# Token-order Q, one store per output block, and dummy matmuls in a convolution and token-mixing kernel

## The chip, the cores and the metric

The kernel runs on one core of one Trainium2 chip. The metric is the device time of one execution in microseconds; the median of three runs stands for a version. The engines are TensorE (PE; PEld is its weight load), VectorE (DVE), ScalarE (ACT), GpSimd (POOL) and SyncE (SP), which here only issues DMAs.

## The reference

Two steps follow one another on x of 8 batches x 4224 tokens x 192 channels (float32).

```python
# 1: causal convolution over 7 tokens, softmax weights, one set per head (24 channels each)
w = exp(weight - max); w = w / sum(w)
x_unf = x_pad[:, idx, :].reshape(B, S, K, H, group)
out = np.einsum('hk,bskhg->bshg', w, x_unf)
# 2: token mixing on that result (call it x again)
wq = x @ w_q;  wk = x @ w_k                       # 192 -> 64
W_tok = scale * np.einsum('bsd,btd->bst', wq, wk) # no softmax, no mask
mixed = np.einsum('bst,btd->bsd', W_tok, x)
out = np.maximum(mixed, 0.0) @ w_out
```

Nothing non-linear stands between the products of step 2, so the kernel never forms the 4224 x 4224 matrix: mixed = Q (w_k^T (x^T x)) scale, with a 192 x 192 Gram matrix per batch.

## The kernel before, in words

Each batch is cut into two halves of HALF = 2112 tokens, and each half into 18 chunks of 120 tokens (the last has 72). One job of each kind, for batch b:

- **Loads** (`load`, lines 192 to 210): GpSimd issues seven DMAs per batch, in three groups of semaphores, which cast x to bf16 on the way; a chunk comes with six tokens ahead of it. First rows and the short last chunks must be zero, which memsets do once (lines 247 to 252 and 359 to 363).
- **Y** (`job_y`, 406): the convolution as a product with a band matrix. Eight jobs per batch: g = 0, 1 is the first or second nine chunks of both halves, hp a pair of heads. Two matmuls of 432 columns, evicted to Y with one instruction, or three.
- **TD** (`job_td`, 449): the Vector engine transposes Y in 32 x 32 blocks, six instructions per batch.
- **Q** (`job_q`, 466): Q^T = w_q^T Y^T, two jobs per batch (g), 48 pairs of matmuls into four PSUM banks. Bank i holds tokens 32 i to 32 i + 31 of every chunk. The evictions (lines 485 to 514) copy bank i as it stands into columns 512 i on of QT: QT is therefore not in token order but has, for each i, all chunks' 32-token pieces behind each other, and the leftovers of the last chunks fill the gaps. Three eviction instructions for g = 0, eight for g = 1.
- **G** (`job_g`, 523): 18 jobs of three matmuls add up the Gram matrix in bank 7. **GEV, TR, MM** (539 to 576) evict it, transpose a part and multiply it with w_k to M.
- **Z** (`job_zd`, `job_zs`, 598 to 626): M times a block of 512 columns of QT (the fifth block is 64), then ReLU into a ring of NZ = 3 buffers.
- **O** (`job_o`, 628): Z times w_out. Output row r of a block takes every fourth column, so a partition holds four successive columns of QT for each half. Two jobs per block fill one buffer of a ring of NO = 8, and `then` (654 to 687) issues its stores. Since QT isn't in token order, a block's 512 columns lie in 16 stretches of 32 tokens: blocks 0 to 2 take one store per half, block 3 three per half (96, 30 and 2 partitions), the rest block one per half. The last block of the run is stored in two parts.

The order is not written out by hand. A planner (lines 697 to 865) holds streams of jobs, estimates when each could start (`ready`: free banks, ends of producers, `x_at` for the loads), and takes the ready job with the lowest due time; a due time is the batch number plus an offset and a slope from KEYS (lines 15 to 18). Each eviction goes to ScalarE or VectorE, whichever the planner's costs say is done first. The result is one fixed instruction list per engine, in which an instruction waits only for its semaphores. `free`, `x_at` and the `end` times set at lines 711 to 720 are the planner's picture of the start: TensorE free at 8.6 us, the third load group of batch 0 there at 12.0, the weights (`wos`) at 12.0. Nothing on the chip corrects them.

At the start TensorE runs 22 matmuls on zeros (`warm`, 388). The Vector engine builds the band matrix (lines 269 to 323), then runs three memsets (`z_later`, 359 to 363), on which GpSimd's loads of batch 1 wait (`load_all(1, z_later)`, 374). Behind those loads GpSimd casts the weights (`wos`, 375 to 386).

Of the kernel before, what the change touches and what calls it, by code (L numbers as in the profile page):

```python
# [12 lines left out]


KEYS = {
    "Y": (-0.34, -0.09), "T": (-0.03, 1.21), "Q": (0.23, 0.82), "G": (-0.01, 0.83),
    "Z": (0.93, 1.25), "O": (1.37, 0.86),
}


# [93 lines left out]
def bass_lightweight_conv__then__hypermixer_token_mlp_kernel(  # L114
# [8 lines left out]
    B, S, D = x.shape  # L123
# [5 lines left out]
    x_t, out_t, w_t = x.tensor, out.tensor, weight.tensor  # L129
# [4 lines left out]
    HALF = S // 2  # L134
    CW = 120
    NCK = 18
    LAST = HALF - 17 * CW
# [11 lines left out]
    P = Program(nc, es)  # L149
# [90 lines left out]
    def dve(fn, deps=()):  # L240
        return P.op("dve", fn, deps)
# [9 lines left out]
    z_band = dve(lambda e: e.memset(BAND[:, :, :], 0.0))  # L251
    z_wall = dve(lambda e: e.memset(WALL[:, :], 0.0))

    load(0, 0, 1, 8, xg[0][0])
    load(0, 1, 0, 9, xg[0][1])
    load(0, 0, 0, 1, xg[0][0], z_first)
# [78 lines left out]
    def twice(ap):  # L335
# [20 lines left out]
        ),  # L356
        [z_id],
    )
    z_later = [
        dve(lambda e: e.memset(shorts[:, 1:], 0.0)),  # L360
        dve(lambda e: e.memset(XW[0:6, 1:, 0, :], 0.0)),
        dve(lambda e: e.memset(ZT[:, :, :, 64:128], 0.0)),
    ]

    def load_all(b, deps):
        load(b, 0, 0, 1, xg[b][0], deps)
# [19 lines left out]
    wos.append(pool(lambda e: e.memset(M_SB[:, :, :], 0.0), [wos[-1]]))  # L386

    def warm(e):
        for i in range(22):
            last = e.matmul(PS[:, 0, :], WARM[:, 0:128], WARM[:, :], start=True, stop=True)  # L390
        return last

# [73 lines left out]
    def job_q(b, g):  # L466


        def pe(e, bk):
            for j in range(6):  # L470
                for i in range(4):
                    r = slice(32 * i, 32 * i + 32)
                    for h in range(2):
                        at_ = 64 * (j // 2 if h == 0 else (4, 5, 3)[j // 2]) + j % 2
                        rhs = YB[r, g, :, at_ : at_ + 63 : 2]
                        last = e.matmul(PS[64 * h : 64 * h + 64, bk + i, 0:288], WQ[r, j, :], rhs,  # L476
                                        start=j == 0, stop=j == 5, skip_group_check=True)
            return last

        def at(i, c):
            return 512 * i + (32 if i < 3 else 24) * c

        n = 9 if g == 0 else 7
        evacs = []
        for i0, i1 in ((0, 2), (2, 3), (3, 4)):

            def make(bk, i0=i0, i1=i1):
                q0 = (b % 2) * HALF  # L490
                w = 32 if i0 < 3 else 24

                def piece(p0, n_, o0, step):

                    if i1 - i0 == 2:
                        return (bass.AP(QT, q0 + o0, [[2 * HALF, 128], [step, 2], [1, n_]]),
                                PS[:, bk + i0 : bk + i1, p0 : p0 + n_])
                    return (QT[:, b % 2, o0 : o0 + n_], PS[:, bk + i0, p0 : p0 + n_])

                if i0 < 3:  # L500
                    r = [piece(0, 32 * n, at(i0, 9 * g), 512)]
                else:
                    o = QT[:, b % 2, at(3, 9 * g) : at(3, 9 * g) + 24 * n]
                    i = PS[:, bk + 3, 0 : 32 * n].rearrange("p (c w) -> p c w", w=32)
                    r = [(o.rearrange("p (c w) -> p c w", w=24), i[:, :, 0:24])]
                if g == 1:
                    r.append(piece(224, w, 1920 + 32 * i0, 32))
                    if i0 == 0:
                        r.append(piece(256, 32, 2048, 32))
                    if i0 == 2:  # L510
                        r.append(piece(256, 8, 2040, 0))
                return r

            evacs.append((make, ("Q", b, g, i0), (i1 - i0) * (n + 2 * g) * 32, False, "copy"))
# [69 lines left out]
    def zspan(i):  # L584
        return (512 * i, 512 if i < 4 else HALF - 2048)

    def zreads(b, i):
        s0, w = zspan(i)
        k = (0, 0, 2, 3, 3)[i]
        q = [("Q", b, 1, 0), ("Q", b, 1, 2)] if i > 2 else []  # L590
        return [("M", b), ("Q", b, 0, k), ("Q", b, 1, k)] + q

    def zring_after(n):
        bb, k = divmod(n - NZ, 5)
# [33 lines left out]
    def job_o(b, i, q):  # L628
        n = nth(b, i)
        zr, orr = n % NZ, n % NO  # L630
        rem = i == 4

        def pe(e, bk):
            kw = dict(skip_group_check=True)
            for j in range(1 if rem else 2):
                r = 2 * q + j
                cols = slice(0, 128) if rem else slice(r, 512, 4)
                o = PS[:, bk + j, :]
                for h in range(2):
                    e.matmul(o[:, 192 * h : 192 * h + 192], ZT[:, zr, h, cols], WO1,  # L640
                             start=h == 0, stop=False, **kw)
                last = e.matmul(o[:, 0:384], ZT[:, zr, 2, cols], WO2, start=False, stop=True, **kw)  # L642
            return last

        def make(bk):
            if rem:
                return [(OUT[0:64, orr, :, 0:192],
                         PS[0:64, bk, 0:384].rearrange("p (h d) -> p h d", h=2))]
            return [(
                OUT[:, orr, :, 384 * q : 384 * q + 384].rearrange("p h (r d) -> p r h d", r=2),  # L650
                PS[:, bk : bk + 2, 0:384].rearrange("p r (h d) -> p r h d", h=2),
            )]

        def then():
# [4 lines left out]
            row = lambda h, t: (b * S + h * HALF + t) * D  # L659
            chunk = [[4 * D, 8], [1, 4 * D]]  # L660
            for h in range(2):
                if rem:
                    parts = [(0, 64, row(h, 17 * CW), [[D, 64], [1, D]])]
                elif halves:
                    parts = [(0, 128, row(h, 32 * i + 2 * q),
                              [[CW * D, 16], [4 * D, 8], [1, 2 * D]])]
                elif i < 3:
                    parts = [(0, 128, row(h, 32 * i), [[CW * D, 16]] + chunk)]
                else:
                    parts = [  # L670
                        (0, 96, row(h, 96), [[CW * D, 16], [4 * D, 6], [1, 4 * D]]),
                        (96, 126, row(h, 16 * CW), [[4 * D, 30], [1, 4 * D]]),
                        (126, 128, row(h, 17 * CW + 64), [[4 * D, 2], [1, 4 * D]]),
                    ]
                for p0, p1, at, dims in parts:
                    src = OUT[p0:p1, orr, h, 0 : D if rem else 4 * D]
                    if halves:
                        src = OUT[:, orr, h, 2 * q * D : 2 * q * D + 2 * D]
                    st = P.dma(
                        "sp",  # L680
                        lambda e, src=src, at=at, dims=dims: e.dma_start(
                            bass.AP(out_t, at, dims), src
                        ),
                        og[orr], evs,
                    )
# [22 lines left out]
    head = {s: 0 for s in streams}  # L708


    free = {"pe": 8.6, "act": 8.5, "dve": 8.8}
    banks = [[0.0, []] for _ in range(8)]
    x_at = {}
    for b in range(B):
        for g in range(3):
            x_at[id(xg[b][g])] = (9.5, 9.5, 12.0)[g] if b == 0 else 3.0 + 9.2 * b + (3.0, 6.0, 9.5)[g]
    for o in band + [ident] + wqs:
        o.end = 8.5
    for o in wos:
        o.end = 12.0  # L720

    def ready(job):
        for r in job.reads:
# [119 lines left out]
    while True:  # L843
# [58 lines left out]
```

## Time and profile before

| | |
|---|---|
| median of three runs | 175.79 us (175.15 to 176.15) |
| profiled execution | 175.42 us |
| its span, first to last instruction | 173.7 us |
| mean granted TensorE clock | 0.964 |
| stores issued by SyncE | 114, 25.95 MB written to HBM |

The 1.7 us between the span and the execution's own time lie around the instructions that the profile shows. In rows of the timeline the first number is the start, the second the length, x the number of merged instructions, and the bracket the idle time of the engine before them with what ended it. A row of the groups ends with busy us and mean ns of one instruction, then idle time before them. A row of a stretch has its length, each engine's busy time and number of instructions, then the granted clock, the busy share of the DMA engines (above one where the transfer times of several queues overlap on an engine) and the rate. Rows of waits end with the sum, the number of times and the longest.

### The profile page before, as it was taken

The page shows a single profiled execution, that of the slowest core. Times are in us where ns is not written, and L with a number is a line of the kernel's source. Part 1 is how long each engine was busy: PE and PEld are TensorE (multiplying, and loading weights), DVE is VectorE, ACT ScalarE, POOL GpSimd, SP SyncE. Part 2 cuts the span into 40 slices and gives each one's busy share as a digit, 9 for nine tenths or more (in the row PEclk, how much of TensorE's full clock was granted, in tenths as well). Part 3 has the DMA queues.
Part 4 walks back from the last instruction along what each step waited for, and adds up shares of the span by engine and source line. Part 5 has one row for each costly group of instructions (what it writes and reads, how often), then busy time and mean ns, then how long its engine had stood idle before and what let it go on. Part 6 is the DMA issues. An engine that isn't in the chain of part 4 may idle for free.

```text
span 173.7 us, 4729 instructions
## 1 busy us (share of the span) xinstructions
PE 152.9 (88%) x1934; PEld 105.5 (61%) x1934; DVE 129.9 (75%) x246; ACT 126.0 (73%) x257; POOL 46.6 (27%) x74
## 2 busy tenths in 40 slices
PE   7755989999989999999999999999999999999400
PEld 2213855776758666766677677757676767766300
DVE  4883969948986899589967997699769976877200
ACT  2562479768987799679966997789768987698500
POOL 7839899999842300000000000000000000000000
PEclk9975999999999999999999999999999999999985
DMA  2999999999999999999999999992859266896697
GB/s 37 185 191 175 191 190 192 190 193 296 265 283 256 280 307 198 313 274 318 226 287 278 310 257 283 281 337 81 251 151 277 70 205 184 225 311 216 204 304 240
DMA packets 48933, 40.43 MB, mean 233 GB/s; under 512 B 39088, under 2 KB 40976, under 8 KB 48912
## 3 DMA queue, kind: packets, MB, share of 16 engines
q0 software_dynamic: 36992, 13.83, 66.9%
q1 hardware_dynamic: 11920, 26.30, 46.1%
q8 instruction: 15, 0.25, 0.5%
q14 instruction: 6, 0.05, 0.1%
HBM read 28.00 MB, written 25.95 MB: 311 GB/s over the span
## 4 chain that ended last, share of the span: by engine, by line
PE 61%; ACT 15%; DVE 9%; POOL 6%; issue 3%; ACTq 0%; POOLq 0%; DVEq 0%
PE ps L413 11%; PE ps L640 10%; PE ps L642 9%; PE ps L476 8%; ACT o_sb L805 6%; ACT zt L808 6%; PE ps L603 6%; PE ps L527 5%; PE ps L528 5%; PE ps L618 3%; PE ps L529 3%; POOL xw L205 3%; ACT y L805 3%; DVE yb L803 2%; DVE y L805 2%
## 5 line engine op out<-in xcount | busy, mean ns | idle before, releaser
L805 ACT COPY o_sb<-ps 128x768 f32<-128x768 f32 (+1 forms) x62 | 46.7, 777 | 6.7 <-PE ps L642 6.2
L640 PE MATMUL ps<-wall,zt 128*128 128x192 bf16 x272 | 45.0, 247 | 0.1
L642 PE MATMUL ps<-wall,zt 128*128 128x384 bf16 x136 | 44.3, 326 | 0.0
L805 ACT CAST y<-ps 128x864 bf16<-128x864 f32 (+3 forms) x58 | 32.5, 617 | 9.0 <-PE ps L413 8.6
L413 PE MATMUL ps<-xw,band 126*128 126x432 bf16 x128 | 32.0, 364 | 5.7 <-DMA xw<-in_x_dram 4.9
L810 DVE TENSOR_SCALAR zt<-ps 128x512 bf16<-128x512 f32 (+1 forms) x47 | 29.2, 634 | 9.6 <-PE ps L603 4.7
L808 ACT ACTIVATE zt<-ps 128x512 bf16<-128x512 f32 (+1 forms) x73 | 33.9, 535 | 1.5 <-PE ps L603 1.4
L640 PEld LDWEIGHTS ps<-wall,zt 128*128 128x128 bf16 x272 | 27.8, 113 | 10.8 <-issue 1.9
L527 PE MATMUL ps<-y 128*128 128x192 bf16 x144 | 34.1, 248 | 0.0
L528 PE MATMUL ps<-y 128*128 128x192 bf16 x144 | 34.0, 247 | 0.0
L803 DVE STREAM_TRANSPOSE yb<-y 128x576 int32<-128x576 int32 x48 | 33.5, 748 | 0.3
L805 DVE CAST y<-ps 128x864 bf16<-128x864 f32 (+3 forms) x38 | 29.7, 815 | 4.6 <-PE ps L413 4.1
L205 POOL DMA_DIRECT2D xw<-in_x_dram x32 | 30.1, 993 | 6.9 <-issue 6.0
L529 PE MATMUL ps<-y 128*128 128x128 bf16 x144 | 31.6, 220 | 0.0
L603 PE MATMUL ps<-qt,m_sb 128*128 128x512 bf16 (+1 forms) x80 | 25.6, 343 | 2.3 <-ACT zt L808 2.1
L805 ACT CAST qt<-ps 128x64 bf16<-128x64 f32 (+4 forms) x34 | 11.8, 403 | 14.3 <-PE ps L476 14.2
L805 DVE CAST qt<-ps 128x224 bf16<-128x224 f32 (+6 forms) x54 | 12.4, 288 | 11.3 <-PE ps L476 11.3
L413 PEld LDWEIGHTS ps<-xw,band 126*128 126x128 bf16 x128 | 10.4, 100 | 16.4 <-ACT band L318 3.1
L528 PEld LDWEIGHTS ps<-y 128*128 128x128 bf16 x144 | 14.2, 99 | 6.7 <-issue 0.2
L527 PEld LDWEIGHTS ps<-y 128*128 128x128 bf16 x144 | 14.2, 98 | 3.2 <-issue 0.4
L476 PE MATMUL ps<-yb,wq 32*64 32x288 bf16 x768 | 15.5, 286 | 0.2 <-DVE yb L803 0.2
L642 PEld LDWEIGHTS ps<-wall,zt 128*128 128x128 bf16 x136 | 15.2, 112 | 0.0
(63 smaller groups left out, 131.6 us busy)
## 6 DMA issues: line engine op xcount, KB each, us to landing
out_dram<-o_sb SPq DMA_DIRECT2D x46, 384.0 KB, 4.4
xw<-in_x_dram POOLq DMA_DIRECT2D x24, 384.0 KB, 19.3
out_dram<-o_sb SPq DMA_DIRECT2D x16, 288.0 KB
xw<-in_x_dram POOLq DMA_DIRECT2D x8, 432.0 KB, 18.0
out_dram<-o_sb SPq DMA_DIRECT2D x16, 90.0 KB
out_dram<-o_sb SPq DMA_DIRECT2D x16, 48.0 KB, 5.6
out_dram<-o_sb SPq DMA_DIRECT2D x4, 192.0 KB
xw<-in_x_dram POOLq DMA_DIRECT2D x16, 29.2 KB, 22.7
```

What stands on the lines that cost most here:

```text
L205: return e.dma_start(XW[0:rows, b % NX, slot : slot + n, :], bass.AP(x_t, base, [[D, rows], [CW * D, n], [1, D]]),)
L413: last = e.matmul(PS[:, k + j, 0:432], BAND[0 : 6 + CW, h, :], rhs, start=True, stop=True)
L476: last = e.matmul(PS[64 * h : 64 * h + 64, bk + i, 0:288], WQ[r, j, :], rhs, start=j == 0, stop=j == 5, skip_group_check=True)
L527: e.matmul(PS[:, 7, 0:192], y[:, 0:128], y[:, 0:192], start=c == 0, **fl)
L528: e.matmul(PS[:, 7, 192:384], y[:, 256:384], y[:, 192:384], start=False, **fl)
L529: return e.matmul(PS[:, 7, 384:512], y[:, 128:256], y[:, 128:256], start=False, **fl)
L603: return e.matmul(PS[:, bk, 0:w], M_SB[:, b % 2, 256 * h : 256 * h + 128], QT[:, b % 2, s0 : s0 + w], start=True, stop=True)
L640: e.matmul(o[:, 192 * h : 192 * h + 192], ZT[:, zr, h, cols], WO1, start=h == 0, stop=False, **kw)
L642: last = e.matmul(o[:, 0:384], ZT[:, zr, 2, cols], WO2, start=False, stop=True, **kw)
L803: last = e.transpose(o, i)
L805: last = e.copy(o, i) if eng == "act" else e.tensor_copy(o, i)
L808: last = e.activation(o, i, AF.Relu)
```

## The change

- QT is written in token order: the evictions of Q spread each bank's 32-token pieces with a stride of 120. Seven eviction instructions per batch instead of eleven. Z of a block then needs Q of the first nine chunks (blocks 0 and 1), of both (block 2), or of the second (3 and 4).
- A block of output is 512 successive tokens of each half, so one store per block takes both halves (two, of half the width, for the last block of the run).
- The two memsets of `z_later` on the x buffers move ahead of the band matrix; the third one stays, and the loads of batch 1 no longer wait for it.
- 32 matmuls on zeros instead of 22 at the start. While no G job has been placed, the planner fills any gap of TensorE over 0.3 us with a matmul on zeros, counted as 0.22 us, which waits for the band matrix.
- KEYS, `free`, `x_at` and the `end` times have other numbers.

```diff
-    "Y": (-0.34, -0.09), "T": (-0.03, 1.21), "Q": (0.23, 0.82), "G": (-0.01, 0.83),
-    "Z": (0.93, 1.25), "O": (1.37, 0.86),
+    "Y": (-0.34, 0.43), "T": (-0.12, 1.03), "Q": (0.02, 0.45), "G": (-0.01, 0.79),
+    "Z": (0.76, 1.54), "O": (1.57, 0.83),
...
     z_wall = dve(lambda e: e.memset(WALL[:, :], 0.0))
+    z_later = [
+        dve(lambda e: e.memset(shorts[:, 1:], 0.0)),
+        dve(lambda e: e.memset(XW[0:6, 1:, 0, :], 0.0)),
+    ]
...
-    z_later = [
-        dve(lambda e: e.memset(shorts[:, 1:], 0.0)),
-        dve(lambda e: e.memset(XW[0:6, 1:, 0, :], 0.0)),
-        dve(lambda e: e.memset(ZT[:, :, :, 64:128], 0.0)),
-    ]
+    dve(lambda e: e.memset(ZT[:, :, :, 64:128], 0.0))
...
-        for i in range(22):
+        for i in range(32):
...
+                n = 9 if g == 0 or i0 == 0 else 8
+                def piece(c, n_, w_):
+                    o = bass.AP(
+                        QT, (b % 2) * HALF + (9 * g + c) * CW + 32 * i0,
+                        [[2 * HALF, 128], [32, i1 - i0], [CW, n_], [1, w_]],
+                    )
+                    i = PS[:, bk + i0 : bk + i1, 32 * c : 32 * c + 32 * n_]
+                    i = i.rearrange("p i (c w) -> p i c w", w=32)[:, :, :, 0:w_]
+                    return (o, i) if i1 - i0 > 1 else (o[:, 0], i[:, 0])
+                r = [piece(0, n, w)]
+                if g == 1 and i0 == 2:
+                    r.append(piece(8, 1, LAST - 64))
...
-        k = (0, 0, 2, 3, 3)[i]
-        q = [("Q", b, 1, 0), ("Q", b, 1, 2)] if i > 2 else []
-        return [("M", b), ("Q", b, 0, k), ("Q", b, 1, k)] + q
+        gs = ((0,), (0,), (0, 1), (1,), (1,))[i]
+        return [("M", b)] + [("Q", b, g, k) for g in gs for k in (0, 2, 3)]
...
+            each, lo, hi = (1, 0, D) if rem else (4, 0, 4 * D)
+            if halves and not rem:
+                lo, hi = 2 * q * D, 2 * q * D + 2 * D
+            rows = 64 if rem else 128
+            to = bass.AP(
+                out_t, (b * S + 512 * i) * D + lo,
+                [[each * D, rows], [HALF * D, 2], [1, hi - lo]],
+            )
+            src = OUT[0:rows, orr, :, lo:hi]
+            st = P.dma("sp", lambda e: e.dma_start(to, src), og[orr], evs)
...
-    free = {"pe": 8.6, "act": 8.5, "dve": 8.8}
+    free = {"pe": 9.9, "act": 9.9, "dve": 9.9}
...
-            x_at[id(xg[b][g])] = (9.5, 9.5, 12.0)[g] if b == 0 else 3.0 + 9.2 * b + (3.0, 6.0, 9.5)[g]
+            x_at[id(xg[b][g])] = (10.0, 10.0, 14.8)[g] if b == 0 else 5.0 + 9.5 * b + (4.0, 6.5, 11.0)[g]
     for o in band + [ident] + wqs:
-        o.end = 8.5
+        o.end = 9.9
     for o in wos:
-        o.end = 12.0
+        o.end = 20.0
...
         s = best[1]
+        if head["G"] == 0 and best[2] > free["pe"] + 0.3:
+            P.op("pe", lambda e: e.matmul(PS[:, 7, :], WARM[:, 0:128], WARM[:, :], start=True,
+                                          stop=True), band)
+            free["pe"] += 0.22
+            continue
         place(streams[s][head[s]], best[2])
```

More of the change, by code (lines that the diff above doesn't have):

```diff
@@ L478, in pe @@
             return last
-        def at(i, c):
-            return 512 * i + (32 if i < 3 else 24) * c
-        n = 9 if g == 0 else 7
         evacs = []
@@ L489, in make @@
             def make(bk, i0=i0, i1=i1):
-                q0 = (b % 2) * HALF
                 w = 32 if i0 < 3 else 24
[L493 to L511, printed above, removed]
-                return r
-            evacs.append((make, ("Q", b, g, i0), (i1 - i0) * (n + 2 * g) * 32, False, "copy"))
+                n = 9 if g == 0 or i0 == 0 else 8
[10 more added lines that the diff above has]
+                    r.append(piece(8, 1, LAST - 64))
+                return r
+            evacs.append((make, ("Q", b, g, i0), (i1 - i0) * (32 if i0 < 3 else 24) * 9, False,
+                          "copy"))
         return Job(
@@ L587, in zreads @@
     def zreads(b, i):
-        s0, w = zspan(i)
-        k = (0, 0, 2, 3, 3)[i]
-        q = [("Q", b, 1, 0), ("Q", b, 1, 2)] if i > 2 else []
-        return [("M", b), ("Q", b, 0, k), ("Q", b, 1, k)] + q
+        gs = ((0,), (0,), (0, 1), (1,), (1,))[i]
+        return [("M", b)] + [("Q", b, g, k) for g in gs for k in (0, 2, 3)]
     def zring_after(n):
@@ L658, in then @@
             evs = [o for k in range(q if halves else 0, q + 1) for o in made[("OUT", b, i, k)]]
[L659 to L685, printed above, removed]
+            each, lo, hi = (1, 0, D) if rem else (4, 0, 4 * D)
[8 more added lines that the diff above has]
+            st = P.dma("sp", lambda e: e.dma_start(to, src), og[orr], evs)
             st.end = max(o.end for o in evs) + 5.0
```

## The prediction

> **What bounds the kernel now.** I read the page first, then busy time by stage, then the two ends of the run in the timeline.
>
> ```profile
> span 173.7 us, 4729 instructions
> PE 152.9 (88%) x1934; PEld 105.5 (61%) x1934; DVE 129.9 (75%) x246; ACT 126.0 (73%) x257; POOL 46.6 (27%) x74
> ...
> core 0: us, PE busy (x) PEld busy (x) DVE busy (x) ACT busy (x) POOL busy (x), PEclk, DMA share, GB/s
> 10.00:15.00 5.00, 2.62 (x9) 0.83 (x10) 3.29 (x5) 1.88 (x4) 3.34 (x5) 0.58 1.38 179
> 15.00:20.00 5.00, 5.00 (x40) 3.63 (x39) 3.50 (x5) 2.76 (x5) 4.49 (x12) 0.73 1.55 189
> 20.00:60.00 40.00, 38.07 (x576) 26.53 (x574) 32.02 (x59) 31.43 (x68) 32.08 (x43) 1.00 1.47 234
> 60.00:150.00 90.00, 88.54 (x1191) 63.50 (x1192) 75.45 (x140) 74.19 (x154) 0.00 (x0) 1.00 1.05 246
> 154.00:159.00 5.00, 4.95 (x38) 2.97 (x36) 4.09 (x9) 4.42 (x10) 0.00 (x0) 1.00 0.90 278
> 159.00:165.00 6.00, 3.45 (x31) 2.62 (x30) 2.14 (x3) 3.82 (x6) 0.00 (x0) 1.00 0.62 182
> 166.00:170.00 4.00, 0.00 (x0) 0.00 (x0) 0.00 (x0) 0.00 (x0) 0.00 (x0) 0.73 0.99 344
> ```
>
> The 88% hides three stages. From 60 to 150 us TensorE is busy 88.54 of 90 us: it is the bound there, and five batches of 18 us leave it 1.46 us idle, 0.29 a batch. From 10 to 20 us it is not: it is idle 2.38 us and its granted clock is 0.58 and then 0.73. At the end no engine computes any more, yet the run goes on for ten microseconds. The stores explain those:
>
> ```profile
> 152.54 1.18 SPq L681 DMA_DIRECT2D out_dram<-o_sb  x2
> 154.29 16.66 SPq L681 DMA_DIRECT2D out_dram<-o_sb  x24
> 165.25 5.70 SPq L681 DMA_DIRECT2D out_dram<-o_sb  x6
> L681 SPq DMA_DIRECT2D out_dram<-o_sb x114: 236/587/1444, 36.2 to 170.4; - x114
> DMA to landing us min/median/max: 3.3/4.9/7.2
> out_dram<-o_sb SPq DMA_DIRECT2D x16, 90.0 KB
> out_dram<-o_sb SPq DMA_DIRECT2D x16, 6.0 KB
> 152.76 1.50 ACT L805 COPY o_sb<-ps 128x768 f32<-128x768 f32 x2 [0.25 <-PE ps L642]
> 156.12 1.53 DVE L805 COPY o_sb<-ps 128x768 f32<-128x768 f32 x2 [0.18 <-PE ps L642]
> 159.81 1.51 ACT L805 COPY o_sb<-ps 128x768 f32<-128x768 f32 x2
> 161.18 0.96 DVE L805 COPY o_sb<-ps 128x768 f32<-128x768 f32 x1 [1.00 <-PE ps L642]
> 161.83 1.50 ACT L805 COPY o_sb<-ps 128x768 f32<-128x768 f32 x2 [0.51 <-PE ps L642]
> ```
>
> The last eviction ends at 161.83 + 1.50 = 163.33, but SyncE issues its last 24 stores without a pause from 154.29 to 170.95. A store occupies it for 0.59 us in the median, hardly less for 90 KB in 30 rows than for a half block of 384 KB. While it works through the many small ones (159 to 165) the DMA engines are 0.62 busy and move 182 GB/s; once only half blocks come (166 to 170) they are 0.99 busy at 344. So the tail is first a queue of issues on SyncE, and only then a transfer at full rate.
>
> **The merged stores.** Per batch 3 x 2 + 6 + 2 = 14 stores become five; the total falls from 114 to 41 (5 x 8, and one more for the halved last block). Bytes and the longest run (four tokens, 3,072 bytes) stay. No row shows an issue of 256 runs. Its bounds are 0.59 us (30 rows cost what 128 do) and twice that, 1.2; I take 0.6, and even 1.2 is under the transfer's own time, so it costs nothing here. Rework the queue with the evictions where they are. A block of 786 KB at 344 GB/s takes 2.29 us, a remainder block of 98 KB 0.29. A half block needs 1.14 us of transfer and lands 3.3 us after its issue at the least, so about 2.2 us are fixed (estimate). Transfers end: batch 6's block 2, issued at 152.54, at 157.0; block 3, ready at 154.26, at 159.3; remainder 159.6; batch 7's block 3, ready at 157.65, at 162.1 (159.85 + 2.29); remainder 162.4; block 0, ready at 160.61, at 165.1; block 1 (162.14) at 167.4; block 2 (162.63 and 163.33) at 169.7. That is 4.0 us before 173.7. The last block goes in runs half as long, so I take 3.7. At 278 GB/s over 0.90 busy, 309, the same chain ends at 170.7: gain 3.0. The best case is a last store that lands 4.9 us after 163.33, at 168.2: 5.5. The bound from below is zero, in the first rival. Earlier in the run the list of waits names no engine that waits for a store (the output ring is eight deep), so the other saved issues count nothing.
>
> **The start.**
>
> ```profile
> 1.25 6.26 PE L390 MATMUL ps<-warm 128*128 128x512 bf16 x22 [1.25 <-DVE warm L247]
> 1.31 2.06 POOL L205 DMA_DIRECT2D xw<-in_x_dram  x2 [0.81 <-POOLq L887]
> 4.30 1.78 POOL L205 DMA_DIRECT2D xw<-in_x_dram  x2
> 2.40 0.51 DVE L252 MEMSET wall<- 128x544 uint32 x1
> 4.40 0.17 DVE L270 TENSOR_TENSOR bits<-bits 128x5 int32<-128x5 int32 x1 [1.49 <-POOL bits L261]
> 9.71 0.86 DVE L360 MEMSET xw<- 128x960 uint32 x1 [0.26 <-issue]
> 10.60 0.46 DVE L361 MEMSET xw<- 6x480 uint32 x1
> 11.07 0.30 DVE L362 MEMSET zt<- 128x288 uint32 x1
> 12.58 1.06 DVE L805 CAST y<-ps 128x864 bf16<-128x864 f32 x1 [0.30 <-PE ps L413]
> 10.14 2.40 PE L413 MATMUL ps<-xw,band 126*128 126x432 bf16 x8 [2.63 <-DMA xw<-in_x_dram]
> 14.78 2.34 PE L413 MATMUL ps<-xw,band 126*128 126x432 bf16 x6 [2.24 <-DMA xw<-in_x_dram]
> 11.66 0.54 POOL L201 DMA_DIRECT2D xw<-in_x_dram  x1 [3.44 <-DVE zt L362]
> 16.93 2.72 POOL L328 CAST wall<-wst 128x192 bf16<-128x192 f32 x7
> ```
>
> TensorE stands idle for 2.63 us after the 22 warm-up matmuls and for 2.24 us until the third load group of batch 0 lands, and works at half clock between and after. Ten more warm-ups cost between the planner's 0.22 each and the mean of the 22, 6.26 / 22 = 0.285: they end at 9.7 to 10.4 instead of 7.51, against a start at 10.14. At worst that is 0.2 late, and 2 us late if they ran at half clock; the wait until 14.78 covers either.
>
> Clock: at 0.73 from 15 to 20 us, 5.00 x 0.27 = 1.35 us are lost on work that TensorE does without a gap; the dummies keep it occupied from 10 to 14.8, and I count 1.35.
>
> Fill: the planner's arrival of the third group goes from 12.0 to 14.8 (real: 14.78), so the Gram matmuls of chunks 0 to 8 are put ahead of the Y jobs of that group. They need all four evictions of the first half, which end at 12.58 + 1.06 = 13.64; with the two memsets gone from 9.71 the Vector engine can begin 0.3 earlier, say 13.3. That leaves 1.5 us before 14.78 for real work: 1.5.
>
> Given back: with work drawn forward, TensorE meets the reduction chain Gram, transpose, M of batch 0 with less to do beside it; it was idle 1.93 of 40 us between 20 and 60 already. I charge 0.6. The start then brings 1.35 + 1.5 - 0.6 = 2.25; bounds 0 (second rival) and 1.35 + 1.5 + 1.0 = 3.85, if half of the 1.93 goes too.
>
> The memsets: 0.86 + 0.46 = 1.32 us move in front of the first `bits` operation, where the Vector engine now idles 1.49 us for GpSimd: free by 0.17 us, and without that cover the band matrix would be up to 1.32 late. GpSimd issues loads at that moment. Two issues beside memsets took 2.06 us, two without 1.78, so I expect 0.1 to 0.3 of delay, inside the estimate of 13.3. [...]
>
> The loads of batch 1 no longer wait 3.44 us. GpSimd passes seven load issues; the weight casts behind them (16.93) wait for weights that SyncE asks for only at 9.6, so they and the loads of batch 2 behind them stay put. The DMA share of 1.38 against 1.55 shows a hole of at most 0.6 us in the load stream that this closes; batch 1 comes that much earlier, with TensorE otherwise occupied. I count nothing, bounds 0 and 0.6.
>
> **The steady part.**
>
> ```profile
> L805 ACT CAST qt<-ps 128x64 bf16<-128x64 f32 (+4 forms) x34 | 11.8, 403 | 14.3 <-PE ps L476 14.2
> L805 DVE CAST qt<-ps 128x224 bf16<-128x224 f32 (+6 forms) x54 | 12.4, 288 | 11.3 <-PE ps L476 11.3
> PEld ps L603 <- ACT zt L808: 3.6, 5, 0.7
> ```
>
> Q's evictions go from 11 to 7 instructions a batch: 88 in 24.2 us now, so four fewer of the short kind save at most 4 x 0.29 = 1.2 us of ScalarE and VectorE per batch. Neither is the bound (75 and 74 of 90 us), so this counts nothing; were they the bound it would be a gain. Writing tokens in runs of 32 instead of whole rows could cost from nothing to the mean of one Q eviction per batch, also covered. The new due times reorder every batch. The ceiling of a gain is the 0.29 idle a batch, 2.0 over seven; no row bounds the loss, which is the third rival. I take 0.4 of gain.
>
> Sum against the profiled execution, 175.42 us (span 173.7 and 1.7 around it): 175.4 - 3.7 - 2.25 - 0.4 = 169.1. The median of the three runs is 175.79, 0.37 above it: 169.4.
>
> **Rivals.** *The tail is bytes, not issues.* For it: from 165.25 on, six issues take 5.70 us, 0.95 each against 0.59, so they are pushed back by full engines. Against it: 159 to 165. If the engines take the two-half stores at the 246 GB/s of the steady part, a block costs 3.2 us and the same chain ends no earlier than now, at 174.7; the gain is nil: 175.8 - 2.65 = 173.1. [...] Chance 0.12.
>
> *The start brings nothing*, because dummies are laid at planned, not real times, or the clock drops anyway, or the lead is lost waiting for batch 1 and the weights: 175.8 - 3.7 - 0.4 = 171.7. The idle 1.93 between 20 and 60 speaks for it. Chance 0.16.
>
> *Slower: the reordering starves TensorE.* Z of a batch is now due at 0.76, but its ring of three buffers is freed by the second output job of block 2 of the batch before, due at 1.57 + 0.83 x 5/9 = 2.03, that is 1.03 on the same scale. Z jobs then come overdue and in bursts of three, and wait for evictions with the output jobs behind them. Now such a wait costs 0.7 us once a batch (3.6 over five). It decides from (3.7 + 2.25) / 7 = 0.85 us more per batch; with two more such waits, 1.4 us, over seven batches the time is 175.8 - 5.95 + 9.8 = 179.6. Against it: the planner only places jobs that are ready, and has other streams to choose. Chance 0.08.
>
> *All of it and more*: idle gone (2.0) and the start at its bound: 175.8 - 3.7 - 3.85 - 2.0 = 166.2. Chance 0.06.
>
> **How the numbers follow.** The forecast has 0.58, at 169.4, its own range 167.4 to 171.4 (tail 3.0 to 5.5, start 1.2 to 3.0). The range 166.4 to 173.0 takes in the second rival and reaches to the edges of the first and of the fastest case. A measurement can tell about 0.5%, 0.9 us, from no change. Faster: 0.58 + 0.12 + 0.16 + 0.06 less 0.01 for a first rival that also loses the start = 0.91; slower 0.06; same 0.03 (a starved order that just eats the gain).
>
> **What would show it.** Right: 41 stores, SyncE waiting again between stores after 154, the last store issued under 1 us behind the last eviction, the DMA engines over 0.9 busy from there to the end, and 5 to 7 us between last eviction and end; clock 1.00 from 10 to 20 us; Gram matmuls before the third load group. Wrong: a tail of 10 us still; issues of 1.2 us or more that follow each other without a pause; a clock of 0.5 between 10 and 18; TensorE idle over 0.5 us per batch between 60 and 140.

## The result and the profile after

The changed kernel takes 166.88 us (median of four runs, 164.21 to 167.47) against 175.97 before; the ratio, from undisturbed runs alone, is 0.9405, 95% interval 0.928 to 0.953. That is faster, and by more than the forecast of 169.4: by the ratio the time is 165.5, below the low end of the range (166.4 to 173.0), while the plain median lies just inside it. The profiled execution took 166.53 us with a span of 164.8, 8.9 less than before.

The head of the changed kernel's page, and its stretches, to be laid beside those of before (length, busy us of each engine, granted clock, DMA share, GB/s):

```profile
span 164.8 us, 4643 instructions
PE 153.1 (93%) x1950; PEld 106.7 (65%) x1950; DVE 123.8 (75%) x232; ACT 127.6 (77%) x239; POOL 46.5 (28%) x74
```

```profile
10.00:15.00 5.00, 4.91 (x37) 2.91 (x38) 4.19 (x6) 1.79 (x4) 3.68 (x5) 1.00 1.57 188
15.00:20.00 5.00, 3.58 (x72) 2.29 (x71) 2.76 (x6) 3.21 (x6) 2.19 (x7) 1.00 1.53 203
20.00:60.00 40.00, 39.04 (x545) 27.11 (x544) 32.99 (x60) 32.83 (x63) 32.31 (x43) 1.00 1.46 233
60.00:140.00 80.00, 78.14 (x1068) 57.08 (x1066) 62.22 (x113) 69.02 (x134) 0.00 (x0) 1.00 1.08 259
150.00:155.00 5.00, 5.00 (x41) 3.41 (x40) 4.58 (x11) 4.49 (x8) 0.00 (x0) 1.00 0.96 356
155.00:160.00 5.00, 3.85 (x33) 2.76 (x31) 2.04 (x3) 4.21 (x6) 0.00 (x0) 1.00 0.99 373
```

The clock is full throughout the first batches, TensorE is occupied from 10 to 15 us, and the DMA engines are 0.96 to 0.99 busy from 150 to 160 us, while there is still computing. The stores and the last evictions, from the timeline and from the tile of the output buffers (durations in ns: min, median, max):

```profile
145.27 15.52 SPq L655 DMA_DIRECT2D out_dram<-o_sb  x11
157.57 2.20 ACT L775 COPY o_sb<-ps 128x768 f32<-128x768 f32 x3 [0.43 <-PE ps L629]
```

```profile
L655 SPq DMA_DIRECT2D out_dram<-o_sb x41: 372/372/983, 37.3 to 159.8; - x41
DMA to landing us min/median/max: 2.3/5.4/8.4
```

There are 41 stores; the last is issued at 159.8, right behind the last eviction (157.57 + 2.20 = 159.77). From there to the end of the span it is 5.0 us, where it was 10.35. The last eviction itself comes 3.55 us earlier than before (163.33). 5.35 and 3.55 make up the 8.9. A merged store costs SyncE 0.372 us, less than a half block did (0.587), not the same or double.

The period of the middle part is read from an instruction that comes once a batch, the eviction of the Gram matrix. Batches 4 and 5 before, then after:

```profile
95.13 0.69 DVE L805 CAST gs<-ps 128x512 bf16<-128x512 f32 x1
113.37 0.69 DVE L805 CAST gs<-ps 128x512 bf16<-128x512 f32 x1
```

```profile
92.79 0.69 DVE L775 CAST gs<-ps 128x512 bf16<-128x512 f32 x1
110.48 0.69 DVE L775 CAST gs<-ps 128x512 bf16<-128x512 f32 x1
```

18.24 us a batch became 17.69. That is 0.55 a batch, where I had put the ceiling at 0.29. And one thing had been in no forecast, a gap in the Gram matmuls of batch 3 that the trace puts down to nothing ("issue"):

```profile
69.54 0.25 PE L516 MATMUL ps<-y 128*128 128x192 bf16 x1
71.64 0.24 PE L517 MATMUL ps<-y 128*128 128x192 bf16 x1 [1.85 <-issue]
```

```profile
q8 instruction: 1, 0.02, 2.1%
```

The last line is of the DMA queues between 69 and 71.7 us: one packet of 0.02 MB (16 KB) on the queue that the profile calls instruction.

### The profile page after: what moved, and what is told of

The parts are those of the page before. It is cut to its first block, busy times and chain, and to the rows that moved or that the text cites. A ratio compares the mean times of both kernels' runs of the same rounds, so it can differ in the third digit from the quotient of the medians.

```text
span 164.8 us, 4643 instructions
## 1 busy us (share of the span) xinstructions
PE 153.1 (93%) x1950; PEld 106.7 (65%) x1950; DVE 123.8 (75%) x232; ACT 127.6 (77%) x239; POOL 46.5 (28%) x74
## 4 chain that ended last, share of the span: by engine, by line
PE 75%; DMA 7%; DVE 4%; ACT 4%; issue 3%; POOL 2%; SPq 2%; ACTq 0%; POOLq 0%
PE ps L627 14%; PE ps L629 13%; PE ps L414 11%; PE ps L590 8%; PE ps L477 8%; PE ps L517 6%; PE ps L516 6%; PE ps L605 4%; DMA xw<-in_x_dram 4%; PE ps L518 4%; DMA wst<-in_moe_w_out_dram 3%; ACT y L775 3%; DVE yb L773 3%; SPq L220 2%; POOL wall L333 1%
## 5 line engine op out<-in xcount | busy, mean ns | idle before, releaser
L775 ACT COPY o_sb<-ps 128x768 f32<-128x768 f32 (+1 forms) x58 | 43.9, 765 | 9.8 <-PE ps L629 7.2
L775 ACT CAST y<-ps 128x864 bf16<-128x864 f32 (+3 forms) x67 | 42.1, 682 | 7.1 <-PE ps L414 7.1
L780 DVE TENSOR_SCALAR zt<-ps 128x512 bf16<-128x512 f32 (+1 forms) x57 | 33.0, 589 | 15.3 <-PE ps L605 8.1
L627 PEld LDWEIGHTS ps<-wall,zt 128*128 128x128 bf16 x272 | 26.7, 113 | 11.4 <-ACT o_sb L775 2.7
L778 ACT ACTIVATE zt<-ps 128x512 bf16<-128x512 f32 (+1 forms) x63 | 30.9, 532 | 0.1
L590 PE MATMUL ps<-qt,m_sb 128*128 128x512 bf16 (+1 forms) x80 | 24.1, 343 | 0.0
L775 DVE CAST y<-ps 128x864 bf16<-128x864 f32 (+3 forms) x29 | 18.7, 679 | 3.1 <-PE ps L414 2.9
L516 PEld LDWEIGHTS ps<-y 128*128 128x128 bf16 x144 | 14.0, 97 | 6.9 <-ACT y L775 1.5
L775 DVE CAST qt<-ps 128x256 bf16<-128x256 f32 (+4 forms) x38 | 11.3, 349 | 9.4 <-PE ps L477 9.4
L517 PEld LDWEIGHTS ps<-y 128*128 128x128 bf16 x144 | 14.1, 98 | 6.6
L775 ACT CAST qt<-ps 128x576 bf16<-128x576 f32 (+2 forms) x18 | 10.8, 610 | 9.5 <-PE ps L477 9.4
L518 PEld LDWEIGHTS ps<-y 128*128 128x128 bf16 x144 | 14.0, 98 | 2.0 <-issue 2.0
L414 PEld LDWEIGHTS ps<-xw,band 126*128 126x128 bf16 x128 | 10.5, 98 | 7.5 <-ACT y L775 1.9
```

The lines of the kernel that those rows point to most:

```text
L414: last = e.matmul(PS[:, k + j, 0:432], BAND[0 : 6 + CW, h, :], rhs, start=True, stop=True)
L516: e.matmul(PS[:, 7, 0:192], y[:, 0:128], y[:, 0:192], start=c == 0, **fl)
L517: e.matmul(PS[:, 7, 192:384], y[:, 256:384], y[:, 192:384], start=False, **fl)
L518: return e.matmul(PS[:, 7, 384:512], y[:, 128:256], y[:, 128:256], start=False, **fl)
L590: return e.matmul(PS[:, bk, 0:w], M_SB[:, b % 2, 256 * h : 256 * h + 128], QT[:, b % 2, s0 : s0 + w], start=True, stop=True)
L775: last = e.copy(o, i) if eng == "act" else e.tensor_copy(o, i)
```

## The experiments

**Theory.** Three gains that act apart: fewer issues cut the tail, the due times shorten the period, the new start brings a little. Rivals: the period comes from token order; the tail is bytes. In the table, "last eviction", "tail" (from there to the end of the span) and "period" (Gram eviction of batch 3 to batch 6, a third; batches count from 0) are read from the profiled execution; the time is the median of its runs, the ratio is to the runs of before on the same chip.

| run | time | ratio to before (95%) | last eviction | tail | period |
|---|---|---|---|---|---|
| before | 175.97 |  | 163.33 | 10.35 | 18.25 |
| changed | 166.88 | 0.941 (0.928 to 0.953) | 159.77 | 5.0 | 17.68 |
| token order and stores alone | 171.50 | 0.980 (0.975 to 0.984) | 164.76 | 5.3 | 18.36 |
| start alone | 174.51 | 0.995 (0.992 to 0.999) | 161.70 | 10.5 | 18.37 |
| due times alone | 172.88 | 0.988 (0.984 to 0.992) | 159.07 | 11.7 | 17.69 |
| all but due times | 168.33 | 0.962 (0.957 to 0.966) | 161.62 | 4.9 | 18.56 |
| a store per half | 167.51 | 0.955 (0.952 to 0.959) | 160.23 | 5.0 | 17.67 |
| no dummies, 22 warm-ups | 164.75 | 0.939 (0.935 to 0.942) | 157.77 | 5.0 | 17.68 |
| old start | 166.18 | 0.948 (0.944 to 0.951) | 159.09 | 5.1 | 17.67 |
| Q jobs apart | 164.83 | 0.940 (0.936 to 0.943) | 157.93 | 4.8 | 17.68 |
| due times of Z and O alone | 179.64 | 1.024 (1.019 to 1.029) | 166.68 | 11.6 | 19.11 |
| due times of Y, T, Q, G alone | 175.44 | 1.000 (0.997 to 1.003) | 162.06 | 11.2 | 18.77 |
| no dummies, Q jobs apart | 164.45 | 0.940 (0.933 to 0.946) | 157.92 | 4.7 | 17.68 |
| no dummies, one warm-up | 169.20 | 0.956 (0.947 to 0.965) | 159.55 | 5.3 | 17.63 |

**Token order and merged stores alone.** To the kernel before, only these hunks of the change: the evictions of Q, `zreads`, and

```diff
-            for h in range(2):
...
+            st = P.dma("sp", lambda e: e.dma_start(to, src), og[orr], evs)
```

> The kernel before with token-order Q, the blocks' reads that go with it and one store per block; due times, start and the planner's picture as before. Theory A (three separate gains: tail from the merged stores 5.3 us, steady period from the due times, a little from the start): period stays 18.2 us a batch, the tail after the last eviction falls from 10.3 to about 5 us, 170 to 171 us in all. Theory B (the shorter period comes from token order itself, since Z waits for less of Q): the period falls to 17.7 as well, 166 to 168 us. Theory C (tail is bytes, gain comes from elsewhere): tail 8 us or more, 174 or more.

171.50 us, tail 5.3, period 18.36, as the first theory had it. The whole gain is in the tail; the last eviction is even 1.4 us later than before (the planner's order came out differently, with batches of 15 to 21 us). Token order gives no shorter period.

```profile
163.26 1.50 ACT L774 COPY o_sb<-ps 128x768 f32<-128x768 f32 x2 [0.51 <-PE ps L628]
150.44 15.41 SPq L654 DMA_DIRECT2D out_dram<-o_sb  x10
```

Ten stores are spread over 15.4 us, where 26 stood one behind the other in 18.4, almost without a pause; the last issue ends at 165.85, 1.1 us behind the last eviction.

**The start alone.** To the kernel before: 32 warm-ups, dummies, the memsets' new place, `free`, `x_at` and `end`.

> The kernel before with the start alone: 32 warm-up matmuls, dummies, memsets moved, the planner's new picture of the start; old Q order, stores and due times. Theory A: the Gram eviction of batch 0 comes 1.5 us earlier, the lead is kept, 174 us. Rival: the lead is given back at the loads and weights before batch 2, 175.3 or more. My prediction's value for the start was 2.25 us, 173.5.

174.51 us, ratio 0.995. In the profiled executions the last eviction comes at 161.70, 1.63 us earlier, and the span is 1.5 us shorter; the medians differ by only 0.74. The Gram eviction of batch 0 comes 3.17 us earlier, twice what theory A said, and about half of that lead is still there at the end. The kernel before, then this one:

```profile
24.94 0.68 DVE L805 CAST gs<-ps 128x512 bf16<-128x512 f32 x1
```

```profile
21.77 0.65 DVE L806 CAST gs<-ps 128x512 bf16<-128x512 f32 x1
```

**The due times alone.** To the kernel before:

```diff
-    "Y": (-0.34, -0.09), "T": (-0.03, 1.21), "Q": (0.23, 0.82), "G": (-0.01, 0.83),
-    "Z": (0.93, 1.25), "O": (1.37, 0.86),
+    "Y": (-0.34, 0.43), "T": (-0.12, 1.03), "Q": (0.02, 0.45), "G": (-0.01, 0.79),
+    "Z": (0.76, 1.54), "O": (1.57, 0.83),
```

> The kernel before with the new due times alone. Theory A: period 17.7 instead of 18.25, but the stores stay many, so the tail stays 10 us: 172 to 173 us. Theory B (token order gives the period): 175 to 176, or slower, since Z of a block still needs both Q jobs.

172.88. The period is 17.69 as after, and the last eviction comes 4.26 us earlier:

```profile
92.06 0.69 DVE L805 CAST gs<-ps 128x512 bf16<-128x512 f32 x1
109.75 0.69 DVE L805 CAST gs<-ps 128x512 bf16<-128x512 f32 x1
...
156.87 2.20 ACT L805 COPY o_sb<-ps 128x768 f32<-128x768 f32 x3 [0.44 <-PE ps L642]
```

But the run gains only 2.9 us of span: SyncE's queue at the end takes 1.3 of the 4.3 back, the tail being 11.7. The two parts need each other.

**All but the due times.** The changed kernel with the two old lines of KEYS.

> The changed kernel with the old due times. Theory A: period 18.2, tail 5, start kept: about 169 to 170 us. Theory B: period 17.7, about 165 to 167 us, as the changed kernel.

168.33, a little under what I wrote, with a tail of 4.9. From batch 3 to batch 7 it takes 72.9 us, 18.2 a batch. Against the changed kernel that is 1.5 us in the medians, and 3.5 against its variants without the gap, below. From "token order and stores alone" this kernel differs by the start only: there the start brings 3.17 us in the medians and 3.14 at the last eviction (164.76 and 161.62).

**One store per half**, two per block:

```diff
-            to = bass.AP(
-                out_t, (b * S + 512 * i) * D + lo,
-                [[each * D, rows], [HALF * D, 2], [1, hi - lo]],
-            )
-            src = OUT[0:rows, orr, :, lo:hi]
-            st = P.dma("sp", lambda e: e.dma_start(to, src), og[orr], evs)
+            for h in range(2):
+                to = bass.AP(
+                    out_t, (b * S + h * HALF + 512 * i) * D + lo,
+                    [[each * D, rows], [1, hi - lo]],
+                )
+                src = OUT[0:rows, orr, h, lo:hi]
+                st = P.dma("sp", lambda e, to=to, src=src: e.dma_start(to, src), og[orr], evs)
```

> The changed kernel with two stores per block, one for each half, as many runs of 3,072 bytes as before and each store 128 rows in token order. If the tail was cut because SyncE issues fewer stores: two issues of 0.4 to 0.6 us are still far under the 2 us that a block's transfer takes, so the tail stays at 5 us and the time within 0.5 us of the changed kernel. If the merged store is also quicker to move (396 against 344 GB/s seen in the two tails): the rate at the end falls back to about 345 and the tail grows to 6.5 us or more, 1.5 to 2 us slower.

167.51, 0.63 above the changed kernel's median where the first theory allowed 0.5 (by their intervals the two are not told apart), and the tail is 5.0. Its 82 stores (min, median, max in ns) and the last stretch:

```profile
L656 SPq DMA_DIRECT2D out_dram<-o_sb x82: 332/433/1792, 38.0 to 162.1; - x82
```

```profile
158.00:164.00 6.00, 1.30 (x12) 0.88 (x10) 0.29 (x1) 2.20 (x3) 0.00 (x0) 0.93 1.00 384
```

The last store starts 1.9 us behind the last eviction (160.23), held back by full DMA engines (longest issue 1.79 us), and they move 384 GB/s at a share of 1.00. So merging the halves is not what cut the tail, and not what raised the rate over the 344 of before: getting rid of the six pieces of block 3 and of stores in 16 stretches was enough. Which of these two did it, no run separates.

**Without dummies.**

```diff
-        for i in range(32):
+        for i in range(22):
...
-        if head["G"] == 0 and best[2] > free["pe"] + 0.3:
+        if False and best[2] > free["pe"] + 0.3:
```

> The changed kernel with 22 warm-up matmuls and no dummies; the planner's picture and the moved memsets stay. If the clock matters: 0.5 granted from about 11 to 18 us, the Gram eviction of batch 0 about 1.2 us later, 1 to 1.5 us slower. Rival: hidden by the load of batch 1 and the weights, under 0.5 us.

Neither came true: 164.75, less than the changed kernel's own median. The Gram eviction of batch 0 comes at 23.39 against 23.49, the clock stays full, and from 60 to 140 us TensorE has no idle time at all:

```profile
10.00:15.00 5.00, 3.61 (x31) 2.33 (x32) 4.19 (x6) 1.79 (x4) 3.68 (x5) 1.00 1.56 189
...
60.00:140.00 80.00, 80.00 (x1124) 58.37 (x1122) 63.30 (x117) 70.56 (x137) 0.00 (x0) 1.00 1.10 266
```

The dummies bring nothing here. What this kernel does not have is the gap at 69.8 us, and its 1.85 us are nearly the whole difference in the last eviction (157.77 against 159.77).

**The old start** under the rest of the change.

> The changed kernel with the old start: 22 warm-up matmuls, no dummies, old place of the memsets, old picture of the start. Token order, merged stores and due times stay. If the gains add: last eviction at 161 us or a little later, tail 5 us, 167.5 to 168.5 us, that is 1.5 us over the changed kernel. If the changed kernel gives its lead back later: the same time within 0.7 us.

166.18; also without the long gap. Against the run without dummies, which differs in the planner's picture and the memsets, the last eviction is 1.3 us later. That, not the dummies, is what the start is worth under these due times. Its 22 warm-ups are those of the kernel before, and TensorE stands idle 1.62 and 2.33 us, yet the granted clock is 1.00 from 10 to 20 us where it was 0.58 and 0.73 before.

**Q jobs further apart.**

```diff
-    "Y": (-0.34, 0.43), "T": (-0.12, 1.03), "Q": (0.02, 0.45), "G": (-0.01, 0.79),
+    "Y": (-0.34, 0.43), "T": (-0.12, 1.03), "Q": (0.02, 0.90), "G": (-0.01, 0.79),
```

> The changed kernel with the second Q job of a batch due later (slope 0.90 instead of 0.45). In the changed kernel's trace TensorE stands still for 1.85 us at 69.8 us and the trace names no releaser; 1.1 us after the second of two Q jobs, each of 96 matmuls with 96 weight loads, and a 16 KB packet of the instruction queue moves in that gap. Theory: TensorE has run out of instructions, because two Q jobs use 384 of them in 3 us. Then Q jobs further apart leave no such stall over 1 us, 164 to 166 us. Rival: a chance event or another wait: a stall as long at another place, or none in this run and the same time; or the period suffers and it is slower.

164.83, no gap of TensorE over 0.5 us after 24 us, last eviction 157.93. The theory's forecast holds, though it counts each Q job double: the trace has 768 matmuls of Q, 48 in each of 16 jobs, so a job has 24 pairs, not 48, and two jobs with their weight loads are 192 instructions, not 384. In the changed kernel the second Q job starts 2.1 us after the first from batch 3 on (65.6 and 67.7), here 3.5 (64.6 and 68.1). Of the waits from 65 to 76 us, the changed kernel and the one with a store per half, which has the same TensorE program, show the same hole:

```profile
PE ps L517 <- issue: 1.9, 1, 1.9
```

```profile
PE ps L517 <- issue: 1.6, 1, 1.6
```

**Half of the due times each.**

```diff
-    "Z": (0.93, 1.25), "O": (1.37, 0.86),
+    "Z": (0.76, 1.54), "O": (1.57, 0.83),
```

The counterpart has the other line of KEYS instead, with Y, T, Q and G.

> The kernel before with only the due times of Z and O changed. In the kernel before, TensorE loses 0.64 us a batch right behind Z matmuls (270 ns from one start to the next against 217 in the changed kernel). If that comes from O following its Z too closely, so that they wait for each other's evictions, the later O takes it away: period 17.7 us, about 172.5 us. If it needs the new times of Y, Q and G: 18.2 and 175 us or more.

> The counterpart: only the due times of Y, Q and G changed, Z and O as before. If Z and O make the period: 18.2 us a batch, about 175 us. If Y, Q and G make it: 17.7 and about 172.5 us. If it takes both, neither run reaches 17.7.

Neither theory held. Z and O alone make the kernel 2.4% slower: the period is 19.12 (94.26 to 113.38), and TensorE waits, in the Z matmuls of line 618, for a bank that an output eviction holds (waits from 60 to 150 us):

```profile
PEld ps L618 <- DVE o_sb L805: 4.5, 4, 1.1
PE ps L618 <- DVE o_sb L805: 2.5, 4, 0.6
```

Y, T, Q and G alone change nothing (ratio 1.000; period 18.77). Only both together give 17.69. The traces say where it is lost: from the Gram eviction of batch 3 to that of batch 6, the next matmul behind a Z matmul of 512 columns starts up to 0.67 us after it in the kernel before, up to 1.00 with Z and O alone, up to 1.42 with Y, T, Q and G alone, and never later than 0.22 with both. Why just this pair avoids those waits is not explained by these runs.

**No dummies and Q jobs apart**, the two edits above together.

> The changed kernel with 22 warm-ups, no dummies and the second Q job due later. If a late code chunk is what costs the changed kernel its 1.9 us, either of the two edits has removed it already, and together they bring no more than the better one: 164.3 to 164.9 us. If they act by other ways, they add up: 163.5 or less.

164.45: no more than either alone. By intervals none of the three is told apart from the others, or from the changed kernel.

**One warm-up matmul, no dummies.**

```diff
-        for i in range(32):
+        for i in range(1):
...
-        if head["G"] == 0 and best[2] > free["pe"] + 0.3:
+        if False and best[2] > free["pe"] + 0.3:
```

> The changed kernel without dummies and with one warm-up matmul instead of 32, so that the clock can't be granted before real work has run for some time. If the clock of the first batch counts on the path: 0.5 granted until 14 us or later, the Gram eviction of batch 0 0.5 to 1.4 us later than without dummies (23.4), 165.5 to 166.5 us. If loads and weights set the first batch: within 0.3 us of 164.75.

That the warm-up begins slowly can be read in the kernel before, where the first six of its 22 matmuls take 607 to 634 ns and the median of the later ones is 379. This run took 169.20, more than expected; the profiled execution took 166.67, 2.15 above the one without dummies (164.52), and the other three 168.99 to 169.43, where no trace shows what was lost. The first eight Y matmuls run slowly, although the column of the granted clock reads 1.00 from 10 to 15 us; this kernel first, then the one without dummies:

```profile
9.98 3.04 PE L414 MATMUL ps<-xw,band 126*128 126x432 bf16 x8 [8.12 <-DVE band L323]
```

```profile
9.97 1.26 PE L414 MATMUL ps<-xw,band 126*128 126x432 bf16 x6 [0.94 <-DVE band L323]
11.47 0.54 PE L414 MATMUL ps<-xw,band 126*128 126x432 bf16 x2 [0.24 <-ACT y L775]
```

The Gram eviction of batch 0 comes 1.09 later (24.48 against 23.39). The other 1.1 is a gap without releaser again, at another place, 36 us, behind two Q jobs 2.5 us apart (31.1 and 33.6); the row is of the waits from 30 to 60 us:

```profile
PE ps L518 <- issue: 1.1, 1, 1.1
```

## Why the prediction was right and wrong

*The tail: right in kind, too small.* The step was "I take 3.7"; it measured 5.35, near the best case of 5.5. The queue on SyncE was the cause, as every run with the old stores (tails of 10.4 to 11.7) and every run with the new (4.7 to 5.3) says. Token order and stores alone keeps the old due times, so its end can be laid beside the chain of the prediction. The largest mis-sized term is the time of a lone merged block: the chain has 2.2 + 2.29 = 4.49 us from issue to landing, but the four blocks that were stored from 136 to 152 us, when the engines were not full, landed after 3.4:

```profile
out_dram<-o_sb SPq DMA_DIRECT2D x4, 768.0 KB, 3.4
```

Batch 7's block 0, where the chain's last queue begins, took 3.44 (issued at 162.07, landed at 165.51). That is 1.05 us. The two blocks behind it took 1.99 and 2.09 instead of 2.29 each, 0.5 more, and the last one's shorter runs did not cost the 0.3 taken off for them. Against these stands 0.5 us from the last landing to the end of the span, which the chain put at nothing: 3.7 + 1.05 + 0.5 + 0.3 - 0.5 = 5.05, and this run's tail is 5.0 shorter. The issue (0.372 instead of 0.6 us) was mis-sized too, but was no term of the sum.

What raised the rate at the end to 356 to 384 GB/s is in part open. It was not the merging of the halves, by the run with a store per half. Nor was it the shorter runs of the last block: of the 453 packets of 512 B and more in the slow stretch of the kernel before (166 to 170 us) 11 are under 2 KB, of the 988 in the quick stretch of the run with a store per half (158 to 164 us) 474 are:

```profile
DMA packets 506, 1.37 MB, mean 344 GB/s; under 512 B 53, under 2 KB 64, under 8 KB 506
```

```profile
DMA packets 1105, 2.30 MB, mean 384 GB/s; under 512 B 117, under 2 KB 591, under 8 KB 1105
```

Packets of 3,072 bytes took 140 ns in the mean in the first and 124 in the second. What the author is left with is the order of the stores' runs in the output; no run tests it alone, so that it is the cause is not shown.

*The start: 2.25 forecast; what it brings depends on the due times.* With the new ones it brought 1.32 us at the last eviction (old start against no dummies), with the old ones 1.63 beside the old stores and 3.14 beside the new. So 2.25 lies among the measured values, but not for the reasons given. The fill was right: Gram matmuls run from 13.17 to 14.7, ahead of the third load group. The charge of 0.6 for what is given back was too small beside the old stores, where 3.17 at batch 0 became 1.63. The 1.35 for the clock rested on a wrong step, that dummies are what keeps it up. Six kernels have the start of before, with its 22 warm-ups and without dummies, and TensorE stands idle for 1.2 to 2.6 us and then for 2.2 to 2.6 in all of them. Two were granted 0.58 from 10 to 15 us (before, due times alone), four 1.00; of these four one fell to 0.66 from 15 to 20 us (token order and stores alone), three did not (old start, and both halves of the due times). So the same start got both clocks; what decides between them these traces do not show. And the loss did not last: due times alone (0.58, then 0.74) and old start (1.00) have the same start and the same due times, and their Gram evictions lie 0.89 us apart in batch 0 (24.55 and 23.66) but 0.08 the other way in batch 3 (74.37 and 74.45), their last evictions 0.02 (159.07 and 159.09). They differ in token order and stores too, so this is a comparison and no test of the clock alone. What the warm-up as a whole is worth is the 1.09 us at batch 0 of the profiled run with one, or more, as that kernel's other runs are slower still.

*The memsets: free; 0.1 to 0.3 us of delay had been expected.* The rows of the changed kernel:

```profile
3.05 0.86 DVE L255 MEMSET xw<- 128x960 uint32 x1
3.35 0.57 POOL L201 DMA_DIRECT2D xw<-in_x_dram  x1
3.96 0.46 DVE L256 MEMSET xw<- 6x480 uint32 x1
4.39 0.17 DVE L275 TENSOR_TENSOR bits<-bits 128x5 int32<-128x5 int32 x1
```

`bits` starts at 4.39 as before (4.40), and GpSimd's issue beside the long memset takes 0.57 us, as it did alone.

*The steady part: the step that failed.* It read "The ceiling of a gain is the 0.29 idle a batch, 2.0 over seven". The due times made the last eviction 4.26 us earlier when they were changed alone, and 3.85 to 5.67 on top of other parts (all but due times against no dummies, token order and stores alone against old start). Each period fell by 0.55, where 0.29 was the ceiling, and 0.4 was taken for the whole run. The step treated the idle time that the profile shows as all there was to win. The idle time was taken from busy time, and a matmul's busy time runs to its modelled end. A Z matmul counts as 381 ns, but two in a row start 217 ns apart in the changed kernel; a wait of up to 0.16 us behind one is counted as work. Two rows of the kernel before show it (the second Z waits for an eviction on ScalarE), and then the same pair in the changed kernel:

```profile
85.66 0.38 PE L603 MATMUL ps<-qt,m_sb 128*128 128x512 bf16 x1
86.33 0.39 PE L603 MATMUL ps<-qt,m_sb 128*128 128x512 bf16 x1 [0.29 <-ACT zt L808]
```

```profile
66.48 0.60 PE L590 MATMUL ps<-qt,m_sb 128*128 128x512 bf16 x2
```

The starts lie 0.67 us apart in the first, of which 0.29 is shown as idle; in the second both matmuls fit into 0.60. From start to start, the twelve Z matmuls of a batch took 3.24 us before and 2.60 after: 0.64, more than the whole difference of the periods, and no other kind of matmul changed by over 0.06. With 0.29 a batch shown as idle, some 0.35 of it had been counted as work (estimate). In the run with the due times alone each of the 27 recorded Z matmuls of these batches is followed after 0.22 us, so the due times are what took the waits away.

*What no rival held: the gap of 1.85 us.* Step by step the last eviction goes from 163.33 to 159.09 (due times, token order, old start), to 157.77 (new start without dummies) and back to 159.77 with the dummies and the gap: 4.24 and 1.32 won, 2.00 lost. That it is a late load of instructions is argued from what the runs show: no releaser, a packet of the instruction queue beside the gap, two Q jobs of 96 instructions each within 3 us ahead of it, and no such gap when Q jobs move apart or when the program in front is 32 instructions shorter. The traces hold two things more. First, the place: the gap comes behind 1,729 recorded TensorE instructions in the changed kernel and in the one with a store per half, and behind 705 in the one with one warm-up, 1,024 apart. Fifteen packets of 16 KB come for the 3,950 recorded instructions of the changed kernel (1,950 matmuls, as many weight loads, 50 of the sequencer), one for 263 if all are TensorE's, which no row tells, so 1,024 is close to four packets (estimate). Second, the time: the three gaps end 1.57, 1.43 and 1.29 us after a packet of that queue has ended (at 70.07, 70.68 and 35.60). In the four kernels where the same place, behind 1,729, passes without a gap, it comes 1.37 to 2.03 us after the packet (old start, no dummies, both edits, Q jobs apart). All of that fits a late packet; but no run changed the queue itself, so the cause stays argued, and why the packet starts as late as it does is open. Runs of one kernel lie 2.3 to 3.3 us apart (changed kernel 164.21 to 167.47, without dummies 164.52 to 167.26, both edits 164.35 to 166.65), and only one of each was profiled: whether the gap is in the other runs is not shown.

*The rivals.* Bytes, not issues: refuted by the tail. Nothing from the start: refuted, 1.3 to 3.1 at the last eviction. Starved by the reordering: with all due times no, with those of Z and O alone yes, at 0.87 us a batch, and near the place I named: Z waits behind output evictions, though for a bank and not for the ring of buffers. All and more, 166.2, which I gave 0.06, came nearest in the number, and that is luck: it has 3.85 for the start, 3.7 for the tail and 2.0 for the steady part, where the runs show 1.3 to 3.1, 5.35 and 3.85 to 5.67, and a gap of 1.85 that took part of it back.

## What to carry to other kernels

Where an engine issues stores without a pause while the DMA engines aren't full (SyncE from 154.29 to 170.95 us, the DMA engines 0.62 busy from 159 to 165), count issues, not bytes: fewer and plainer stores took 5 us off the end of a 174 us run, and until that was done, 1.3 of the 4.3 us that the due times won ahead of it vanished in the same queue. The idle time of TensorE that the profile showed, 0.29 us a batch, was no ceiling for what another order brought, 0.55; compare starts of the same matmul at its quickest and as it is (0.22 and 0.67 us between two Z matmuls here). The due times belonged together: both lines alone gave a ratio of 0.988, one half 1.000, the other 1.024.

## What the hardware showed that was not expected

- A store of 256 runs occupied SyncE for 0.372 us, one of 128 runs in token order 0.433 (median with waiting ones), one of 128 runs in 16 stretches 0.587.
- Stores alone reached 384 GB/s at a DMA share of 1.00; the kernel before 344 at 0.99.
- In three kernels TensorE stood 1.1 to 1.9 us without a releaser in the profile, behind two Q jobs with 192 instructions, until 1.3 to 1.6 us after a packet on the instruction queue; with 16 matmuls and their loads less far ahead of it, the gap of 1.85 us was gone.
- The clock granted from 10 to 15 us differs between six kernels of the same start, 0.58 in two and 1.00 in four, with 22 warm-up matmuls that take 6.25 to 7.41 us.
- The column of the granted clock read 1.00 from 10 to 15 us where eight Y matmuls took 3.04 us behind one warm-up; behind 22, six took 1.26.
